# Loads and stores of turns 16 to 30 issued by ScalarE in place of SyncE, in a softmax-attention decode kernel with its gradients

## Chip, cores and metric

The kernel runs on one core of a Trainium2 chip. The metric is the device time of one execution in microseconds (us), the median of several runs. The core has TensorE (PE; its weight loads are PEld), VectorE (DVE), ScalarE (ACT), GpSimd (POOL) and SyncE (SP), and 16 DMA engines that move data between device memory (HBM) and on-chip memory (SBUF). A DMA is issued by an instruction on one of the engines, here `dma_start` on SyncE or ScalarE, and then runs by itself. An engine executes its instructions in order; one that waits for a semaphore holds up all that stand behind it on the same engine.

## What is computed

One query row per head attends to 8192 keys, for 32 heads of width 128, in bf16; the outputs are the attention result and the gradients with respect to q, k and v.

```python
# q, grad_out: [1, 32, 1, 128]; k, v: [1, 32, 8192, 128]; bf16
def _fwd_reference(q, k, v):
    scale = q.shape[-1] ** -0.5
    scores = jnp.einsum('bhqd,bhkd->bhqk', q, k) * scale
    attn = _softmax(scores, axis=-1)
    return jnp.einsum('bhqk,bhkd->bhqd', attn, v)

def reference(q, k, v, grad_out):
    _out, _vjp = jax.vjp(_f, q, k, v)      # _f: _fwd_reference on q, k, v
    return (_out, *_vjp(grad_out))         # out, dq, dk, dv
```

For a head with attention row p and output gradient g this is: out = p V; dp = V g; ds = scale * p * (dp - sum(p * dp)); dq = ds K; dk = outer(ds, q); dv = outer(p, g). K and V are read once (134 MB in all) and dk and dv, of the same size, are written.

## The kernel before

Per head, K, V, dk and dv are each one SBUF tile of 128 partitions x 64 rows x 128 values: 2 MB, 16 KB of neighbouring memory for each partition. Each is one DMA, except K of head 0 (four parts) and the gradients of the first and last head (two halves). There are three K buffers, two V buffers, two buffers for dk (`G_dk`) and two for dv (`G_dv`).

The main loop (L293) makes 33 turns; turn h does the forward part of head h and the gradient of q and k of head h-1 (`p_`). The program has the order of the work written out by hand (`manual_schedule`, L93), so each engine executes its share in the order in which the loop names it. The steps of a turn:

- `rows_bc` (L256) spreads the rows of q and g over the partitions; ScalarE copies them to `qd` (L263).
- `k_blocks` (L150) transposes K in 32x32 blocks on VectorE, `Kt` to `XK_sb` (L155), the first VectorE work of a turn; `k_scores` (L166) multiplies with q on TensorE.
- `ds_of` (L265) makes ds of head h-1 (L268, L270). `outer(p_, "dk", r)`, r = 0 to 3, makes a quarter of dk on VectorE each (L244). `dq_of` (L274, matmuls L221) makes dq in two halves; ScalarE copies the sum to `w_sb` (L228), and `blocks` (L234) and a copy to `dq_all` (L282) finish it.
- Then `load_k(h + 2)` is issued (L314, the DMA is L76): its buffer is that of head h-1, which the second half of `dq_of` reads last.
- The maximum of the scores, `e` = exp and its sum on ScalarE (L333), the sum over partitions (L334), the reciprocal on VectorE (L341) and the scaled `p_rep` on ScalarE (L343). The last quarter of dk stands between, and with it the store of dk of head h-1 (L254).
- `v_transposes` (L191, matmuls L197) turns V in four parts, which ScalarE copies to `XT_sb` (L188); `v_scores` (L209) makes dp; `wide` (L221) and `blocks` (L234) make out, copied at L354.
- `outer(h, "dv", r)`, four quarters of dv on VectorE (L244); before the last of them `load_v(h + 2)` is issued (L364, the DMA is L80), whose buffer is that of V of head h. Behind the last comes the store of dv of head h (L254).

So the DMAs of a turn are, in order: load of K(h+2), store of dk(h-1), load of V(h+2), store of dv(h). SyncE issues all of them and has nothing else to do; each issue waits there until its buffer is free or its data is ready, and the ones behind it wait with it. ScalarE issues one DMA in all, that of `grad_out` (L84). The K and V tiles of heads 0 to 2 are loaded in the prologue and turn 0.

Of the kernel before, what the change touches and what calls it, by code (L numbers as in the profile page):

```python
# [17 lines left out]
K_BUFS = 3  # L18
V_BUFS = 2
QD = 32  # L20


@with_exitstack
def kernel(
# [11 lines left out]
    nc = tc.nc  # L36
# [4 lines left out]
    NCH = NT // CH  # L41
    NQ = P // QD
    assert NCH == 4 and NQ == 4
    W = D // 2
    NB = W // QD
    scale = float(D) ** -0.5
# [15 lines left out]
    Kt, Vt, XK, XV, st = {}, {}, {}, {}, {}  # L62

    def rows_of(x, h, c, parts):
        L = NT // parts
        return x[0, h].rearrange("(p n) d -> p n d", p=P)[:, c * L:(c + 1) * L, :]

    def slots(X, c, parts):
        L = NT // parts
        return X[:, c * L:(c + 1) * L, :]  # L70

    def load_k(h):
        Kt[h] = kpool.tile([P, NT, D], BF16, tag="K", name="Kt")
        parts = NCH if h == 0 else 1
        for c in range(parts):
            nc.sync.dma_start(slots(Kt[h], c, parts), rows_of(k, h, c, parts))  # L76

    def load_v(h):
        Vt[h] = vpool.tile([P, NT, D], BF16, tag="V", name="Vt")
        nc.sync.dma_start(Vt[h][:], rows_of(v, h, 0, 1))  # L80

    rows = consts.tile([H, 2, D], BF16)
    nc.sync.dma_start(rows[:, 0, :], q.rearrange("b h s d -> (b h s) d"))
# [20 lines left out]
    q_blk = consts.tile([P, H, 2 * NB, NQ], BF16)  # L104
    four = consts.tile([H, 2 * NB, NQ, QD], BF16)
    for w in range(NB):
        for e2 in range(2):
            nc.vector.tensor_copy(
                four[:, 2 * w + e2], rows[:, 0, :].rearrange("h (w j e) -> h w e j", w=NB, e=2)[:, w, e2:e2 + 1, :]
                .to_broadcast([H, NQ, QD]))  # L110
    tp = psT.tile([P, CH, P], BF16, tag="T", name="tp_q")
    for c in range(2 * NB):
        nc.tensor.transpose(tp[:, c, 0:H], four[:, c].rearrange("h a j -> h (a j)"), ident[0:H, 0:H])
    lane = consts.tile([P, QD], F32)
    nc.vector.reduce_sum(lane[:], ident[:].rearrange("p (a i) -> p i a", a=NQ), axis=AX.X)
# [4 lines left out]
    nc.vector.reduce_sum(  # L120
        diag_low[:], ident_f[:, 0:3 * QD].rearrange("p (a k r) -> p k r a", a=3, r=R)[:, 0:R, 0, :], axis=AX.X)
    diag = consts.tile([P, R], F32)
# [27 lines left out]
    def k_blocks(h, u):  # L150


        if u == 0:
            XK[h] = ktpool.tile([P, CH, NB, NCH, QD], F32, tag="XK", name="XK_sb")
        nc.vector.transpose(XK[h][:, :, :, u, :],  # L155
                            slots(Kt[h], u, NCH).rearrange("p g d -> p (g d)").bitcast(F32).rearrange(
                                "p (g w j) -> p g w j", g=CH, w=NB))

    def k_scores(h):
        x = st[h]  # L160
        out = x["s"][:, 0:NT].rearrange("p (a g) -> p g a", a=NQ)
        cols = XK.pop(h).rearrange("p g w u i -> p (g w u i)").bitcast(BF16).rearrange(
            "p (g w ui e) -> p g w e ui", g=CH, w=NB, e=2)
        for g in range(CH):
            for c in range(2 * NB):
                nc.tensor.matmul(out[:, g, :], lhsT=cols[:, g, c // 2, c % 2], rhs=q_blk[:, h, c, :],  # L166
                                 start=(c == 0), stop=(c == 2 * NB - 1), skip_group_check=True)
# [69 lines left out]
    def outer(h, which, r):  # L237
        x = st[h]
        if r == 0:
            x[which] = gpool.tile([P, NT, D], BF16, tag=which, name="G_" + which)  # L240
        G, dst = x[which], out_2 if which == "dk" else out_3
        rep, row = x["ds"] if which == "dk" else x["p"], x["qd"][:, 0 if which == "dk" else 1, :]
        Q = NT // 4
        nc.vector.tensor_tensor(  # L244
            slots(G, r, 4).rearrange("p n (a b) -> p n a b", b=R),
            slots(rep, r, 4).unsqueeze(2).to_broadcast([P, Q, D // R, R]),
            row.rearrange("p (a b) -> p a b", b=R).unsqueeze(1).to_broadcast([P, Q, D // R, R]),
            op=ALU.mult)
        parts = 1
        if h == 0 or h == H - 1:  # L250
            parts = 2
        if r % (4 // parts) == 4 // parts - 1:
            c = r // (4 // parts)
            nc.sync.dma_start(rows_of(dst, h, c, parts), slots(G, c, parts))  # L254

    def rows_bc(h):  # L256
        x = st[h]
        x["s"] = psS.tile([P, 512], F32, tag="s", name="s_ps")
        nc.tensor.matmul(x["s"][:, 256:512], lhsT=ident[0:H, h:h + 1].to_broadcast([H, P]),
                         rhs=rows[:].rearrange("h a d -> h (a d)"), start=True, stop=True,  # L260
                         skip_group_check=True)
        x["qd"] = small.tile([P, 2, D], BF16, tag="qd", name="qd")
        nc.scalar.copy(x["qd"][:].rearrange("p a d -> p (a d)"), x["s"][:, 256:512])  # L263
# [10 lines left out]
    def dq_of(h, half):  # L274
        wide(h, "dq", half * NT // 8, (half + 1) * NT // 8)
        if half == 1:
            wide_out(h)

    def dq_out(h):
        out = st[h]["dp"][:, 128:129]  # L280
        blocks(h, out)
        nc.scalar.copy(dq_all[:, h:h + 1], out)  # L282
# [10 lines left out]
    for h in range(H + 1):  # L293
        p_ = h - 1
        if h < H:
            x = st[h] = {}
            rows_bc(h)
            for u in range(NCH):
                k_blocks(h, u)
            k_scores(h)  # L300
        if h == 0:
            do_columns()
        if h > 0:
            ds_of(p_)
            outer(p_, "dk", 0)
            dq_of(p_, 0)
        if h < H:
            s_mask(h)
            s_swap(h)
        if h > 0:  # L310
            dq_of(p_, 1)
            outer(p_, "dk", 1)
        if 0 < h and h + 2 < H:
            load_k(h + 2)  # L314
        if h < H:
            mx = small.tile([P, 1], F32, tag="mx")
            nc.vector.reduce_max(mx[:], x["sn"], axis=AX.X)
            top = small.tile([P, 1], F32, tag="top")
            nc.vector.tensor_scalar_mul(top[:], mx[:], scale)  # L319
            x["m"] = psM.tile([P, 512], F32, tag="m", name="m_ps")  # L320
            nc.tensor.transpose(x["m"][:, 128:256], top[:].to_broadcast([P, P]), ident_f[:])  # L321
        if h > 0:
            outer(p_, "dk", 2)
            dq_out(p_)
        if h == 0:
            load_k(2)
        if h < H:
            nbias = small.tile([P, 1], F32, tag="nbias")
            nc.vector.tensor_reduce(nbias[:], x["m"][:, 128:256], axis=AX.X, op=ALU.max, negate=True)
            v_transposes(h, 0, copy=False)  # L330
            e = small.tile([P, NT], F32, tag="e")
            rs = small.tile([P, 1], F32, tag="rs")
            nc.scalar.activation(e[:], x["sn"], ACT.Exp, bias=nbias[:], scale=scale, accum_out=rs[:])  # L333
            nc.tensor.matmul(x["m"][:, 0:1], lhsT=ones_f[:], rhs=rs[:], start=True, stop=True,  # L334
                             skip_group_check=True)
        if h > 0:
            outer(p_, "dk", 3)
        if h == H:
            break
        rinv = small.tile([P, 1], F32, tag="rinv")  # L340
        nc.vector.reciprocal(rinv[:], x["m"][:, 0:1])  # L341
        x["p"] = small.tile([P, NT, R], BF16, tag="prep", name="p_rep")
        nc.scalar.activation(x["p"][:], e[:].unsqueeze(2).to_broadcast([P, NT, R]), ACT.Copy, scale=rinv[:])  # L343
        x["p_s"] = small.tile([P, NT], F32, tag="p_s", name="p_s")
        nc.vector.tensor_scalar(x["p_s"][:], e[:], rinv[:], scale, op0=ALU.mult, op1=ALU.mult)
        v_copy(h, 0)
        v_transposes(h, 1)
        v_transposes(h, 2)
        wide(h, "o", 0, NT // 4)
        wide_out(h)  # L350
        v_scores(h, 0)
        v_scores(h, 1)
        blocks(h, x["m"][:, 2:3])
        nc.scalar.copy(o_all[:, h:h + 1], x["m"][:, 2:3])  # L354
        v_transposes(h, 3)
        nc.tensor.matmul(x["m"][:, 1:2], lhsT=do_f[:, h:h + 1].to_broadcast([P, P]), rhs=o_all[:, h:h + 1],
                         start=True, stop=True, skip_group_check=True)
        v_scores(h, 2)
        v_scores(h, 3)
        outer(h, "dv", 0)  # L360
        outer(h, "dv", 1)
        outer(h, "dv", 2)
        if 0 < h and h + 2 < H:
            load_v(h + 2)  # L364
        outer(h, "dv", 3)
        if h == 0:
            load_v(2)
        if h == H - 1:
            result(o_all, out_0)
# [33 lines left out]
```

## Time and profile before

| | |
|---|---|
| median of 3 runs | 648.34 us (648.29 to 648.54) |
| profiled execution | 648.14 us, span 646.3 us |
| busy: PE, PEld | 528.0 us (82%), 423.2 us (65%) |
| busy: DVE, ACT | 506.1 us (78%), 214.5 us (33%) |
| moved by DMA | 269.49 MB, mean 417 GB/s |
| mean granted clock of TensorE | 0.684 of full speed |

The span runs from the first to the last instruction of the profiled execution; the rest of that execution's time lies around it. The page of the profile gives the busy time of each engine, a row of 40 slices of the span with the busy share in tenths, the DMA queues with their packets, bytes and share of the 16 engines' span, and the DMA issues by line with the median time from issue to landing. Queue q1 is that of SyncE, q10 that of ScalarE, q8 and q14 fetch instructions. Further views of the same trace: the chain of work that ended last, followed back from the end and shown in order of time (start, duration, what); the waits of an engine (line, what it waited for, total, times, longest); the timeline of one engine (start, duration, instruction, and in brackets the idle time before it with what ended it), where "SPq" marks an instruction that SyncE's sequencer issues; and a table by stretch of time (busy time of PE, PEld, DVE, ACT and POOL with the number of instructions, then granted clock, DMA share and GB/s).

### The profile page before, as it was taken

To read this page: it belongs to the slowest core of one execution; us is meant where nothing else is said; L and a number is where in the kernel's file an instruction comes from. 1 tells how busy PE (TensorE), PEld (TensorE's weight loads), DVE (VectorE), ACT (ScalarE), POOL (GpSimd) and SP (SyncE) were. 2 spreads that over 40 slices of the span, in tenths; PEclk is the share of its full clock that TensorE was granted. 3 is DMA by queue.
4 is the path that set the end of the run, shared out by engine and by line. 5 is a ranking of instruction groups with operands and counts; after the bars stand their busy time and mean duration, and the time that the engine had idled before them with its cause. 6 is when DMAs were issued, how large, how long until landed. Compare 5 with 4: busy or idle time off the path is not lost.

```text
span 646.3 us, 15913 instructions
## 1 busy us (share of the span) xinstructions
PE 528.0 (82%) x7113; PEld 423.2 (65%) x7113; DVE 506.1 (78%) x655; ACT 214.5 (33%) x396; POOL 0.7 (0%) x6
## 2 busy tenths in 40 slices
PE   3988998889899987889877898877897788977781
PEld 3677776766777766667665776656675666766570
DVE  5988888889888778877788777797777977778861
ACT  2334333333343332343313333223432334332340
POOL 0000000000000000000000000000000000000000
PEclk9877665677776656777567765667765777656775
DMA  8999999999999999999999999999999999999984
GB/s 354 399 428 426 425 425 428 424 425 427 427 430 426 429 427 426 429 429 427 429 426 428 428 431 426 427 429 425 429 429 427 427 428 429 427 427 425 423 358 189
DMA packets 19700, 269.49 MB, mean 417 GB/s; under 512 B 2352, under 2 KB 2352, under 8 KB 2864
## 3 DMA queue, kind: packets, MB, share of 16 engines
q1 hardware_dynamic: 19584, 268.47, 98.0%
q8 instruction: 56, 0.92, 0.6%
q14 instruction: 12, 0.10, 0.0%
q10 hardware_dynamic: 48, 0.01, 0.0%
HBM read 134.23 MB, written 134.23 MB: 415 GB/s over the span
## 4 chain that ended last, share of the span: by engine, by line
DMA 49%; DVE 24%; PE 22%; ACT 2%; issue 1%; SPq 0%; ACTq 0%; DVEq 0%
DMA Kt<-in_k_dram 49%; DVE XK_sb L155 15%; DVE G_dv L244 8%; PE w_ps L221 6%; PE s_ps L166 6%; PE T_ps L197 4%; PE dp_ps L234 3%; ACT w_sb L228 1%; ACT p_rep L343 1%; PE s_ps L182 1%; PE m_ps L334 0%; DVE rinv L341 0%; PE dp_ps L209 0%; DVE pdt L268 0%; ACT XT_sb L188 0%
## 5 line engine op out<-in xcount | busy, mean ns | idle before, releaser
L197 PE MATMUL T_ps<-ident_f,Vt 128*128 128x128 f32 x1024 | 202.8, 365 | 1.6 <-ACT XT_sb L188 1.3
L197 PEld LDWEIGHTS T_ps<-ident_f,Vt 128*128 128x128 f32 x1024 | 180.1, 206 | 12.1 <-ACT XT_sb L188 12.1
L244 DVE TENSOR_TENSOR G_dv<-p_rep,qd 128x2048 bf16<-128x2048 bf16 x128 | 148.2, 1220 | 30.5 <-DMA out_dram<-G_dv 27.5
L244 DVE TENSOR_TENSOR G_dk<-ds_rep,qd 128x2048 bf16<-128x2048 bf16 x128 | 155.7, 1218 | 1.1
L155 DVE STREAM_TRANSPOSE XK_sb<-Kt 128x1024 f32<-128x1024 f32 x128 | 148.2, 1213 | 4.9 <-DMA Kt<-in_k_dram 4.6
L188 ACT COPY XT_sb<-T_ps 128x1024 f32<-128x1024 f32 x128 | 128.6, 1008 | 44.5 <-PE T_ps L197 40.8
L166 PE MATMUL s_ps<-q_blk,XK_sb 128*128 128x4 bf16 x2048 | 59.7, 168 | 70.0 <-DVE pdt L268 63.3
L166 PEld LDWEIGHTS <-XK_sb 128*128 128x128 bf16 x2048 | 56.9, 104 | 76.8 <-DVE pdt L268 69.9
L228 ACT COPY w_sb<-w_ps 128x512 f32<-128x512 f32 x64 | 37.6, 587 | 175.5 <-PE w_ps L221 175.4
L209 PEld LDWEIGHTS <-XT_sb 128*128 128x128 bf16 x2048 | 60.7, 98 | 36.9 <-ACT XT_sb L188 23.3
L209 PE MATMUL dp_ps<-do_blk,XT_sb 128*128 128x2 bf16 x2048 | 65.5, 164 | 20.5 <-ACT XT_sb L188 20.5
L234 PEld LDWEIGHTS dp_ps<-diag,w_sb 128*128 128x128 f32 x256 | 56.9, 327 | 17.3 <-ACT w_sb L228 17.3
L221 PE MATMUL w_ps<-Kt,ds_rep 128*32 128x512 bf16 x512 | 67.1, 625 | 0.4 <-DVE ds_rep L270 0.4
L234 PE MATMUL dp_ps<-diag,w_sb 128*128 128x1 f32 x256 | 59.7, 354 | 7.3 <-ACT w_sb L228 7.3
L341 DVE RECIPROCAL rinv<-m_ps 128x1 f32<-128x1 f32 x32 | 5.4, 168 | 70.1 <-PE m_ps L334 70.1
L343 ACT ACTIVATE p_rep<-e,rinv 128x256 bf16<-128x256 f32 x32 | 16.2, 507 | 58.0 <-DVE rinv L341 58.0
L221 PE MATMUL w_ps<-Vt,p_rep 128*32 128x512 bf16 x512 | 34.0, 386 | 0.0
L234 PE MATMUL m_ps<-diag,w_sb 128*128 128x1 f32 x256 | 33.0, 250 | 0.0
L234 PEld LDWEIGHTS m_ps<-diag,w_sb 128*128 128x128 f32 x256 | 31.0, 191 | 0.0
L282 ACT COPY dq_all<-dp_ps 128x1 f32<-128x1 f32 x32 | 5.1, 159 | 62.5 <-PE dp_ps L234 62.5
L321 PEld LDWEIGHTS m_ps<-ident_f,top 128*128 128x128 f32 x32 | 5.8, 182 | 29.0 <-DVE top L319 29.0
L182 PEld LDWEIGHTS s_ps<-sm,lane 128*32 128x32 f32 x256 | 10.4, 151 | 17.5 <-DVE sm L172 16.6
(51 smaller groups left out, 220.9 us busy)
## 6 DMA issues: line engine op xcount, KB each, us to landing
Vt<-in_v_dram SPq DMA_DIRECT2D x32, 2048.0 KB, 29.3
Kt<-in_k_dram SPq DMA_DIRECT2D x31, 2048.0 KB, 31.1
out_dram<-G_dv SPq DMA_DIRECT2D x30, 2048.0 KB, 34.0
out_dram<-G_dk SPq DMA_DIRECT2D x30, 2048.0 KB, 33.8
out_dram<-G_dv SPq DMA_DIRECT2D x4, 1024.0 KB, 15.0
out_dram<-G_dk SPq DMA_DIRECT2D x4, 1024.0 KB, 13.4
Kt<-in_k_dram SPq DMA_DIRECT2D x4, 512.0 KB, 5.2
out_dram<-fin_sb SPq DMA_DIRECT2D x2, 8.0 KB, 12.9
```

The lines of the kernel that those rows point to most:

```text
L155: nc.vector.transpose(XK[h][:, :, :, u, :], slots(Kt[h], u, NCH).rearrange("p g d -> p (g d)").bitcast(F32).rearrange("p (g w j) -> p g w ...
L166: nc.tensor.matmul(out[:, g, :], lhsT=cols[:, g, c // 2, c % 2], rhs=q_blk[:, h, c, :], start=(c == 0), stop=(c == 2 * NB - 1), skip_group ...
L182: nc.tensor.matmul(x["s"][a * QD:(a + 1) * QD, 128:128 + NT], lhsT=lane[:], rhs=x["sm"][:, a].rearrange("p u g -> p (u g)"), start=True, s ...
L188: nc.scalar.copy(X[:], st[h].pop("T")[:])
L197: nc.tensor.transpose(T_ps[:, i, :], words[:, m * P:(m + 1) * P], ident_f[:])
L209: nc.tensor.matmul(st[h]["dp"][:, n:n + 2], lhsT=X[:, i, e2, :], rhs=do_blk[:, h, e2, :], start=(e2 == 0), stop=(e2 == 1), skip_group_chec ...
L221: nc.tensor.matmul(x["w"][a * QD:(a + 1) * QD, :], lhsT=rep[:, n:n + 2 * R, :].rearrange("p n r -> p (n r)"), rhs=Xt[:, 4 * g:4 * g + 4, : ...
L228: nc.scalar.copy(x["wsb"][:].rearrange("p k d -> p (k d)"), x.pop("w")[:])
L234: nc.tensor.matmul(out_col, lhsT=X[:, k, :], rhs=diag[:, k:k + 1], start=(k == 0), stop=(k == R - 1), skip_group_check=True)
L244: nc.vector.tensor_tensor(slots(G, r, 4).rearrange("p n (a b) -> p n a b", b=R), slots(rep, r, 4).unsqueeze(2).to_broadcast([P, Q, D // R, ...
L321: nc.tensor.transpose(x["m"][:, 128:256], top[:].to_broadcast([P, P]), ident_f[:])
L343: nc.scalar.activation(x["p"][:], e[:].unsqueeze(2).to_broadcast([P, NT, R]), ACT.Copy, scale=rinv[:])
```

## The change

A function `issuer(turn)` chooses the engine that issues a DMA: ScalarE for turns 16 to 30, SyncE for all others. The loads and the stores of a turn pass it the number of the turn in which they are issued: h for K and V loads and for the store of dv, and p_ + 1 for the store of dk of head p_. The place of each issue in the program's order stays.

```diff
+FROM, TO = 16, 31
...
-    def load_k(h):
+    def issuer(turn):
+
+        return nc.scalar if FROM <= turn < TO else nc.sync
+
+    def load_k(h, turn=0):
...
-            nc.sync.dma_start(slots(Kt[h], c, parts), rows_of(k, h, c, parts))
-
-    def load_v(h):
+            issuer(turn).dma_start(slots(Kt[h], c, parts), rows_of(k, h, c, parts))
+
+    def load_v(h, turn=0):
         Vt[h] = vpool.tile([P, NT, D], BF16, tag="V", name="Vt")
-        nc.sync.dma_start(Vt[h][:], rows_of(v, h, 0, 1))
+        issuer(turn).dma_start(Vt[h][:], rows_of(v, h, 0, 1))
...
-            nc.sync.dma_start(rows_of(dst, h, c, parts), slots(G, c, parts))
+            issuer(h + 1 if which == "dk" else h).dma_start(rows_of(dst, h, c, parts), slots(G, c, parts))
...
-            load_k(h + 2)
+            load_k(h + 2, h)
...
-            load_v(h + 2)
+            load_v(h + 2, h)
```

## The prediction

> **What bounds the kernel now.** First the page: the DMA row and the queues.
>
> ```profile
> DMA  8999999999999999999999999999999999999984
> q1 hardware_dynamic: 19584, 268.47, 98.0%
> q8 instruction: 56, 0.92, 0.6%
> Vt<-in_v_dram SPq DMA_DIRECT2D x32, 2048.0 KB, 29.3
> out_dram<-G_dk SPq DMA_DIRECT2D x30, 2048.0 KB, 33.8
> ```
>
> The DMA engines are full from the second slice on, nearly all through SP's queue q1. A 2 MB transfer lands some 30 us after its issue, so about six stand in line. Next the chain and the timelines of SP and VectorE, to see how compute hangs on that line:
>
> ```profile
> 206.99 4.53 DVE XK_sb L155 x4
> 294.49 31.18 DMA Kt<-in_k_dram
> 325.69 4.62 DVE XK_sb L155 x4
> ...
> 305.60 0.34 SPq L80 DMA_DIRECT2D Vt<-in_v_dram  x1
> 306.04 0.40 SPq L254 DMA_DIRECT2D out_dram<-G_dv  x1
> 314.42 0.34 SPq L76 DMA_DIRECT2D Kt<-in_k_dram  x1
> 316.81 0.33 SPq L254 DMA_DIRECT2D out_dram<-G_dk  x1
> 325.53 0.34 SPq L80 DMA_DIRECT2D Vt<-in_v_dram  x1
> 334.33 0.34 SPq L76 DMA_DIRECT2D Kt<-in_k_dram  x1
> ...
> 320.85 4.63 DVE L244 TENSOR_TENSOR G_dv<-p_rep,qd 128x2048 bf16<-128x2048 bf16 x4 [1.33 <-DMA out_dram<-G_dv]
> ```
>
> Up to about 207 us a turn takes 18.55 us (chain entries of L155 at 188.50 and 206.99) and the line grows; from then on compute waits for it: K of head 17 (K17) is issued at 294.49, lands at 325.67, and turn 17 starts there. The period is 334.33 - 314.42 = 19.91 us, four transfers of 4.98. Last the end:
>
> ```profile
> SPq L398 <- DMA out_dram<-fin_sb: 12.3, 1, 12.3
> ...
> 630.00:635.00 5.00, 1.78 (x9) 1.51 (x8) 1.90 (x2) 0.63 (x3) 0.00 (x0) 0.50 0.97 402
> 635.00:640.00 5.00, 0.00 (x0) 0.00 (x0) 0.00 (x0) 0.00 (x0) 0.00 (x0) 0.50 0.45 187
> ```
>
> Compute is over at 632.6; SP then waits 12.3 us for the line to empty. So the transfers set the end: it moves later by any time in which the slowest DMA engine has nothing to do, or if compute ends so late that the last store misses the end of the line. The share of 0.45 says that some of the 16 engines finish well before the last one. The profiled execution took 648.14 (span 646.3 and 1.84 around it), the median 648.34; I add differences to the median.
>
> **The change, part by part.** Moved from SP to ScalarE: 14 K loads, 14 V loads, 15 stores of G_dk and 15 of G_dv, 58 issues. Nothing else changes.
>
> *Issue cost.* 0.33 to 0.42 us each on SP; ScalarE's one issue in the trace (grad_out, at 0.73) took 0.42. ScalarE is 33% busy. Where the issues fall in its order:
>
> ```profile
> 334.33 0.59 ACT L228 COPY w_sb<-w_ps 128x512 f32<-128x512 f32 x1 [6.42 <-PE w_ps L221]
> 336.87 0.16 ACT L282 COPY dq_all<-dp_ps 128x1 f32<-128x1 f32 x1 [1.95 <-PE dp_ps L234]
> 336.93 0.32 ACT L333 ACTIVATE e<-s_ps,nbias 128x64 f32<-128x64 f32 x1
> 337.14 0.20 ACT L333 ACTIVATION_READ_ACCUMULATOR e<-s_ps,nbias 128x1 f32 x1
> 339.16 0.51 ACT L343 ACTIVATE p_rep<-e,rinv 128x256 bf16<-128x256 f32 x1 [1.82 <-DVE rinv L341]
> ```
>
> The K load comes behind the w_sb copy and waits for the same matmuls (L221), in the 1.95 us before dq_all. The G_dk store comes behind the read of e's sum and waits for the fourth G_dk multiply (done 336.7), in the 1.82 us before p_rep, which waits for a reciprocal that stands behind that multiply on VectorE anyway. The V load and the G_dv store come behind the last XT copy (ends 326.60); behind them stands the qd copy (327.54), then 6.42 us of idle time. So no wait is added on the path: 58 x 0.4 = 23 us of ScalarE's idle time, price 0. Were that cover gone, it would be 0.4 per turn at p_rep, 15 x 0.4 = 6 us. The transfers themselves start later: K by 0.6, G_dk by 0.6, V and G_dv by 1.1 us. Deep in a line of 30 us that is nothing; with the line empty it counts.
>
> *The crossing at turn 16.* SP's ring holds what was issued before: G_dv14, K17, G_dk14, V17, G_dv15. ScalarE's transfers come through another ring. Do they stand behind SP's line? The fetches of instructions (q8) come in another ring too, 56 times, yet the chain shows 0% of PEq and 1% of issue: they don't wait 30 us. So I let the two rings share, half and half. The numbers on the latest engine, with 1 us from issue to start (an estimate: the 8 KB load of q landed 1.7 us after its issue):
> - K18 starts at about 316. SP's ring then has 24.4 us (G_dv15 landed at 340.7 before); at half speed it lasts till 365.
> - G_dv14 lands at 325 instead of 320.8 and K17 at 335 instead of 325.7. Turn 17 starts 9.6 us late.
> - G_dk14 frees its buffer at 345; VectorE would want it at 340.6. V17 lands at 355 (wanted 351). G_dv15 lands at 365 (wanted 358). Turn 18 starts at about 370 instead of 345.5: compute has lost 24.4 us.
> - ScalarE's ring meanwhile got K18, G_dk15, V18, G_dv16, K19 (ready 350) and G_dk16 (353): 6 x 4.98 = 29.9 us, of which it moved 24.4. At 365 there are 5.4 us left; V19 (ready 366) lasts till 375, G_dv17 (371) till 380.3, K20 (380.3) comes just in time, G_dk17 lasts till 390.2, and V20 is ready at 370 + 19.8 + 1.1 + 1 = 391.8. So the line runs dry for **1.6 us**, 1.1 of which is ScalarE's later issue. Then it grows by 19.91 - 18.55 = 1.36 us per turn.
>
> *The end.* Turn 31 starts at 369.9 + 13 x 18.55 = 611.05 (before 604.82). The last 1 MB store, issued at 631.93 before, goes at about 638.2 and needs 2.5 us and about 1 to start: 641.7, ahead of the line's end (645.2 + 1.6). From turn 31 SP issues again, and G_dk30 (622.1) shares with G_dk29 and G_dv30. G_dk29, 4.9 us of work, lands by 632 and VectorE wants its buffer at 633.5: free.
>
> Sum: 0 + 1.6 + 0 = +1.6: **649.9 us**.
>
> The Trainium skill (DMA: Bandwidth & Descriptors, Rules for kernel authors) says that spreading DMAs over the issuing engines brings no bandwidth, only issue time. SP's four issues take 1.4 of a turn's 19.9 us, so by that rule the time would be 648.3; my 1.6 us come from the order at the crossing, of which the rule doesn't speak. The same page (Queues, rings and completion order) has each DMA engine take its rings in turn, packet by packet, which is the halving assumed above.
>
> *What the trace can't show:* what two full rings do to an engine's rate. Nearest rows: a packet of q1 takes 0.98 x 16 x 646.3 / 19584 = 0.52 us for 13.7 KB (0.62 per 16 KB); a fetch through the other ring 0.006 x 16 x 646.3 / 56 = 1.1 us per 16 KB. Upper end: each of the 80 packets of the shared stretch (2 x 24.4 / 0.61) costs 1.1: +39 us, of which 5 are covered by the slack of the last store: 648.3 + 34 = 682. Lower end: 0, or a small gain (below). I take 0, since the fetch ends in another kind of memory and q1's loads and stores alternate at the full 427 GB/s.
>
> **The rivals.**
> - *Faster: the engines come level again.* The share is 0.90, 0.91, 0.85, 0.83, 0.97, 0.45 in the 5 us stretches from 610 to 640 and 0.05 in the last 6: one engine is late, others are idle. A line that runs nearly dry lets the early ones wait, and the late one may not fall behind again. Bound: not before the last store, 641.7, so 645.2 - 641.7 = 3.5 us less: 644.8 to 647. It decides if lateness comes from a long line rather than from the engine. Against it: nothing shows why that engine is late.
> - *No change, 648.3.* The line never runs dry: 1.6 us is 0.4% of the times it is taken from, and half a transfer more in it at 380 removes it; or rings are served in order of issue.
> - *Two rings cost rate:* 651 to 682 as above; each tenth off the rate in the shared 49 us costs 4.9 on the line.
> - *ScalarE held up:* should an issue there wait longer than the 1.4 us left before p_rep, each further 0.1 us is 1.5 over 15 turns: about 652.
>
> **How the numbers follow.** Dry line 649.9, own range 649.2 to 651: 0.33. No change or under 1.3 us: 0.27. Faster: 0.17. Rate: 0.18. Held up: 0.05. A difference of 0.2% (1.3 us) is what a measurement of this kernel can tell. Slower: 0.18 + 0.05 + three quarters of 0.33 = 0.48; same: 0.27 + 0.08 = 0.35; faster 0.17. The range leaves out the better half of "faster" (below 646.0) and the worse half of "rate" (above 656): 0.17 together.
>
> **What would show it.** In the chain and waits of after: one gap of 4 to 10 us each before L155 (K17), the first G_dk multiply of turn 17, the first T_ps of turn 17 and G_dv of turn 17, all between 320 and 366; none for DMA from turn 18 to 30, which have periods of 18.55; the time to landing near 10 us at turn 19 and growing; a dip in GB/s near 390. p_rep still ends its wait by rinv. The prediction is wrong if K17 lands on time (no sharing), if the GB/s fall between 316 and 365, or if turns 18 to 30 don't run at 18.55.

## The result, and the profile after

The changed kernel takes 653.25 us (median of 4 runs, 652.92 to 653.45), beside 648.44 for the kernel before on the same chip (4 runs). The ratio is 1.0073 with a 95% interval of 1.0055 to 1.009: 4.8 us slower, where 1.6 us had been forecast. The profiled execution took 652.92, of which the span is 651.1.

All line numbers in `kernel.py` are 5 higher than before, because of the added lines: L155 has become L160, L244 L249, L254 L259 and L398 L403.

First the page of the kernel after. The GB/s row has 40 slices of 16.3 us; the queue rows give packets, megabytes and share of the DMA engines' time; the last rows give transfers, KB each and the median time from issue to landing.

```profile
GB/s 352 402 430 423 424 429 425 426 425 429 428 428 425 429 429 429 424 431 429 429 426 429 374 310 398 420 424 427 428 424 428 427 430 425 428 428 427 430 423 206
q1 hardware_dynamic: 11232, 146.83, 53.3%
q10 hardware_dynamic: 8400, 121.65, 44.6%
...
Vt<-in_v_dram ACTq DMA_DIRECT2D x14, 2048.0 KB, 18.9
Kt<-in_k_dram ACTq DMA_DIRECT2D x14, 2048.0 KB, 19.6
out_dram<-G_dk ACTq DMA_DIRECT2D x15, 2048.0 KB, 22.4
out_dram<-G_dv ACTq DMA_DIRECT2D x15, 2048.0 KB, 24.9
```

ScalarE's transfers do have a queue of their own, q10, which now carries nearly half of the work. The slices 23 to 25 (358 to 407 us) show 374, 310 and 398 GB/s: this is the dip that had been placed "near 390", and it is wide. The kernel before has 428, 431 and 426 there.

Now VectorE's timeline of the kernel after. Columns: start, duration, the instruction, and in brackets the idle time ahead of it with what ended it. Only the starts of turns 17 to 19 and the groups that waited for a DMA are shown.

```profile
323.29 4.63 DVE L249 TENSOR_TENSOR G_dv<-p_rep,qd 128x2048 bf16<-128x2048 bf16 x4 [3.76 <-DMA out_dram<-G_dv]
333.00 4.62 DVE L160 STREAM_TRANSPOSE XK_sb<-Kt 128x1024 f32<-128x1024 f32 x4 [5.08 <-DMA Kt<-in_k_dram]
342.99 1.23 DVE L249 TENSOR_TENSOR G_dk<-ds_rep,qd 128x2048 bf16<-128x2048 bf16 x1 [4.74 <-DMA out_dram<-G_dk]
362.83 4.63 DVE L249 TENSOR_TENSOR G_dv<-p_rep,qd 128x2048 bf16<-128x2048 bf16 x4 [7.31 <-DMA out_dram<-G_dv]
367.38 4.62 DVE L160 STREAM_TRANSPOSE XK_sb<-Kt 128x1024 f32<-128x1024 f32 x4
385.93 4.62 DVE L160 STREAM_TRANSPOSE XK_sb<-Kt 128x1024 f32<-128x1024 f32 x4
```

And TensorE's, the first transposes of V in turn 17:

```profile
352.76 1.97 PE L202 MATMUL T_ps<-ident_f,Vt 128*128 128x128 f32 x8 [4.31 <-DMA Vt<-in_v_dram]
```

These are the five waits for SP's half-served line. Turn 18 starts at 367.4 instead of 345.5, so compute has lost 21.9 us; turn 19 follows 18.55 us later and waits for no transfer. The chain of waits of the kernel after says the same. Columns: start, us, what.

```profile
274.58 31.18 DMA Kt<-in_k_dram
305.83 46.88 DMA Vt<-in_v_dram
355.52 7.22 another core or an unknown queue
367.46 4.53 DVE XK_sb L160 x4
386.02 4.53 DVE XK_sb L160 x4
404.58 4.53 DVE XK_sb L160 x4
```

V17 was on its way for 46.88 us, instead of the 30 us usual for SP's line; after the crossing the chain runs through compute at 18.56 us a turn. (The piece put down to an unknown queue ends where G_dv of turn 17 starts; VectorE's timeline above names the transfer.)

The packet records of this trace show the sharing itself. Of the 16 KB packets that start from 317.5 to 342.5 us, 333 go through q1 and 321 through q10; from 342.5 to 360 us it is 97 and 359. One thing more differs from before: SP's last store ahead of the crossing, G_dv15, is issued at 310.91 instead of 306.04, because SP, by its waits, stands 4.7 us for a landing of G_dk. It still stands behind V17 and lands one transfer at half rate after it (352.8 and 362.8), so no effect of this is seen.

Where the lost time is can be read from stretches of 5 us. Columns: the stretch, its length, busy time of PE, PEld, DVE, ACT and POOL with instructions, PE's clock, the share of time in which the 16 DMA engines were busy, and GB/s. Kernel after:

```profile
360.00:365.00 5.00, 3.34 (x61) 3.04 (x57) 2.17 (x2) 1.17 (x2) 0.00 (x0) 0.97 0.78 295
365.00:370.00 5.00, 0.00 (x0) 0.00 (x0) 5.00 (x6) 0.37 (x1) 0.00 (x0) 0.50 1.03 423
370.00:375.00 5.00, 2.95 (x84) 2.39 (x88) 4.72 (x7) 0.00 (x0) 0.00 (x0) 0.50 0.87 367
375.00:380.00 5.00, 4.78 (x29) 3.58 (x22) 3.34 (x6) 1.05 (x4) 0.00 (x0) 0.50 0.71 239
380.00:385.00 5.00, 4.84 (x64) 3.80 (x63) 4.04 (x6) 3.92 (x5) 0.00 (x0) 0.82 1.02 334
385.00:390.00 5.00, 3.48 (x62) 3.09 (x58) 5.00 (x5) 1.56 (x4) 0.00 (x0) 0.86 1.02 377
390.00:395.00 5.00, 4.39 (x89) 2.63 (x89) 4.68 (x9) 0.43 (x1) 0.00 (x0) 0.50 0.96 313
```

Two things lower the rate. From 360 to 365 and from 370 to 380 the share is 0.71 to 0.87: some engines have nothing to do. From 380 to 395 the share is back at 0.96 to 1.02, but the rate is only 313 to 377 GB/s: the engines are busy and move less. By the packet records, 29% of the 16 KB packets that start from 380 to 395 us take more than 0.8 us, against 0.5% from 320 to 360 us; the median is 0.61 us in both stretches.

Why some engines run out first can be read from the landings, of which the trace records 16 for each transfer (one for each engine, as I take it). Around 311 us the first and the last of the 16 lie 8.8 to 8.9 us apart in both kernels. With the line served at half rate this doubles: SP's last transfer, G_dv15, has its landings from 343.9 to 362.7 us. So the first engines are through SP's line 19 us ahead of the last one, go on at full rate with ScalarE's, and reach its end first: the landings of G_dk16 run from 360.4 to 370.1, but the next transfer, V19, is issued only at 362.23. At 418 us the 16 landings of a transfer are 2.7 us apart, against 11.1 before.

The same view in longer stretches gives the balance; the kernel before:

```profile
320.00:360.00 40.00, 32.55 (x447) 26.09 (x446) 31.48 (x40) 13.44 (x25) 0.00 (x0) 0.67 1.01 427
360.00:400.00 40.00, 33.50 (x447) 26.95 (x445) 31.48 (x40) 13.41 (x25) 0.00 (x0) 0.67 1.01 429
400.00:600.00 200.00, 164.54 (x2223) 131.75 (x2222) 157.42 (x200) 66.05 (x122) 0.00 (x0) 0.67 1.01 428
600.00:660.00 60.00, 26.45 (x354) 20.64 (x354) 25.65 (x30) 11.94 (x23) 0.00 (x0) 0.71 0.58 245
```

and after:

```profile
320.00:360.00 40.00, 20.52 (x279) 15.68 (x278) 15.65 (x20) 9.85 (x16) 0.00 (x0) 0.61 1.01 428
360.00:400.00 40.00, 28.57 (x395) 23.32 (x392) 31.37 (x41) 9.72 (x21) 0.00 (x0) 0.64 0.92 346
400.00:600.00 200.00, 177.69 (x2425) 141.67 (x2423) 170.78 (x218) 71.45 (x128) 0.00 (x0) 0.69 1.01 426
600.00:660.00 60.00, 32.00 (x378) 25.41 (x377) 26.91 (x33) 13.84 (x28) 0.00 (x0) 0.67 0.72 303
```

From 320 to 360 the two rings share and the rate is 428 GB/s, as with one. From 360 to 400 the line is short of (429 - 346) / 428 x 40 = 7.8 us of full work. The share falls from 1.01 to 0.92, which accounts for 3.6 us of engines without work; the other 4.2 are engines that are busy and move less. From 400 to 600 another (428 - 426) / 428 x 200 = 0.9 is missing. These 8.7 us are pushed past 600. At the end some comes back: before, 245 x 60 / 428 = 34.3 us of full work took the 45.2 us to the end of the line at 645.2, so 10.9 were lost to engines that finished early; after, 303 x 60 / 428 = 42.5 us of work took 50.0 us, so 7.5 were lost. 8.7 - 3.4 = 5.3 us, beside 4.8 measured. Both kernels move the same bytes, so such a balance has to come out near the measured time; it says where work was lost, not why.

The last landing of each transfer, taken in order and compared with before, says when the end moved: 0.4 us earlier at 370 us, 1.3 later at 387, 2.7 later at 418, 4.7 later at 585, and 4.8 at the end of the line (650.0 and 645.2). So 3.1 us arise between 370 and 418 us, and 2.1 more come slowly over the next 170 us, while the landings of a transfer spread out again from 2.7 to 7.8 us.

The end itself, in SP's timeline of the kernel after, and the wait for the line in its waits:

```profile
627.71 2.60 SPq L259 DMA_DIRECT2D out_dram<-G_dv  x2
637.83 2.60 SPq L259 DMA_DIRECT2D out_dram<-G_dk  x2
640.53 0.41 SPq L296 DMA_DIRECT2D out_dram<-fin_sb  x1
```

```profile
SPq L403 <- DMA out_dram<-fin_sb: 9.1, 1, 9.1
```

The last stores go into a line that still runs for 9.1 us (12.3 before): the transfers, not compute, set the end here too.

### The profile page after: what moved, and what is told of

It is laid out like the page before. It is cut to its first block, busy times and chain, and to the rows that moved or that the text cites. A ratio compares the mean times of both kernels' runs of the same rounds, so it can differ in the third digit from the quotient of the medians.

```text
span 651.1 us, 15890 instructions
## 1 busy us (share of the span) xinstructions
PE 529.7 (81%) x7113; PEld 423.7 (65%) x7113; DVE 504.9 (78%) x655; ACT 214.5 (33%) x396; POOL 0.7 (0%) x6
## 4 chain that ended last, share of the span: by engine, by line
DVE 36%; PE 29%; DMA 27%; ACT 4%; another core or an unknown queue 1%; issue 1%; SPq 0%; DVEq 0%; ACTq 0%
DVE XK_sb L160 18%; DVE G_dv L249 16%; DMA Kt<-in_k_dram 15%; PE s_ps L171 7%; DMA Vt<-in_v_dram 7%; PE w_ps L226 7%; PE T_ps L202 6%; PE dp_ps L239 6%; DMA out_dram<-G_dk 5%; ACT w_sb L233 2%; ACT p_rep L348 2%; PE s_ps L187 1%; PE m_ps L339 1%; DVE rinv L346 1%
## 5 line engine op out<-in xcount | busy, mean ns | idle before, releaser
L202 PEld LDWEIGHTS T_ps<-ident_f,Vt 128*128 128x128 f32 x1024 | 180.5, 206 | 16.3 <-ACT XT_sb L193 11.9
L249 DVE TENSOR_TENSOR G_dv<-p_rep,qd 128x2048 bf16<-128x2048 bf16 x128 | 148.2, 1220 | 26.6 <-DMA out_dram<-G_dv 20.3
L249 DVE TENSOR_TENSOR G_dk<-ds_rep,qd 128x2048 bf16<-128x2048 bf16 x128 | 155.7, 1218 | 9.7 <-DMA out_dram<-G_dk 8.7
L160 DVE STREAM_TRANSPOSE XK_sb<-Kt 128x1024 f32<-128x1024 f32 x128 | 148.2, 1213 | 6.7 <-DMA Kt<-in_k_dram 6.6
L348 ACT ACTIVATE p_rep<-e,rinv 128x256 bf16<-128x256 f32 x32 | 16.3, 508 | 62.5 <-DVE rinv L346 62.5
L287 ACT COPY dq_all<-dp_ps 128x1 f32<-128x1 f32 x32 | 5.1, 159 | 62.5 <-PE dp_ps L239 60.6
```

The costliest lines, as they stand in the source:

```text
L160: nc.vector.transpose(XK[h][:, :, :, u, :], slots(Kt[h], u, NCH).rearrange("p g d -> p (g d)").bitcast(F32).rearrange("p (g w j) -> p g w ...
L202: nc.tensor.transpose(T_ps[:, i, :], words[:, m * P:(m + 1) * P], ident_f[:])
L249: nc.vector.tensor_tensor(slots(G, r, 4).rearrange("p n (a b) -> p n a b", b=R), slots(rep, r, 4).unsqueeze(2).to_broadcast([P, Q, D // R, ...
```

## The experiments

Each is the changed kernel with the edit shown; `FROM` and `TO` are the turns between which ScalarE issues (`TO = 40`: to the end). The kernel before took between 648.12 and 648.23 us beside them, and every ratio is to it.

**ScalarE from the start to the end.** ScalarE issues still more of the transfers, but there is no change of ring while the line is long.

```diff
-FROM, TO = 16, 31
+FROM, TO = 1, 40
```

> FROM, TO = 1, 40: ScalarE issues from turn 1 to the end, so the only crossing lies in turn 1, where the line of transfers is short (about 10 us in place of 25). Theory 'crossing': the loss comes from the new ring overtaking a long line, not from who issues; 648.4 us, between 647.7 and 649.2, XK_sb of turn 17 starts near 325.7 as before. Rival 'issuer': the 4.8 us of turns 16 to 30 are 0.32 us per turn of work held up on ScalarE; with 32 turns 648.4 + 10 = 658.

Measured 646.63 us, ratio 0.9977 (0.9967 to 0.9986): 1.6 us faster than before, and 6.6 faster than the change. The stretch of the dip, in the view by stretches of this kernel:

```profile
360.00:400.00 40.00, 32.75 (x446) 26.06 (x444) 31.48 (x40) 13.40 (x25) 0.00 (x0) 0.67 1.01 429
```

Turn 17 starts at 325.40 after a wait of 0.19 us. So ScalarE as an issuer costs nothing here; the rival by which it does (658) is refuted. The gain had not been expected; its cause stays open.

**One turn on ScalarE.** Only turn 16's four issues cross.

```diff
-FROM, TO = 16, 31
+FROM, TO = 16, 17
```

> FROM, TO = 16, 17: only the four transfers of turn 16 (K18, G_dk15, V18, G_dv16) go through ScalarE's ring. Theory 'crossing': K17, G_dk14 and V17 land as late as with turns 16 to 30 on ScalarE (333, 343, 353 us); G_dv15 about 360 in place of 362.7, since ScalarE's ring is empty after 20 us of work; compute is 2 to 3.5 us earlier, the dry stretch near 380 shorter or gone: 648.5 to 651. Rival 'issuer': one turn of 15 is left: 648.7, and no gaps in turn 17.

Measured 652.06, ratio 1.0064 (1.005 to 1.0077), above what was expected. The waits are nearly those of the full change (K17 5.09, G_dk14 4.72, G_dv15 4.98 us) and the stretch 360 to 400 has 373 GB/s. Four issues out of 58 make 3.8 of the 4.8 us: the price is of the crossing, not of the turns that follow. (The return to SP comes in turn 17 here, while SP's old line is still there; this run doesn't tell the two crossings apart.) By the view by stretches, the share from 360 to 400 us is 0.97, so most of this run's dip is busy engines that move less.

**The crossing late.**

```diff
-FROM, TO = 16, 31
+FROM, TO = 28, 31
```

> FROM, TO = 28, 31: the same crossing 12 turns later, with three turns on ScalarE. Theory 'crossing': turn 30 starts 21.9 us late, as turn 18 did; one turn gives back 1.4 us, so the last store is issued near 652.4 in place of 631.9 and lands 3.5 us later: 11 us more than before, 659 (656 to 662). Rival 'issuer': 3 turns x 0.32 us: 649.4.

Measured 659.42, ratio 1.0175 (1.0161 to 1.0189), as expected. The same waits, three of them here from VectorE's timeline of this kernel:

```profile
572.21 4.62 DVE L160 STREAM_TRANSPOSE XK_sb<-Kt 128x1024 f32<-128x1024 f32 x4 [5.08 <-DMA Kt<-in_k_dram]
582.26 1.22 DVE L249 TENSOR_TENSOR G_dk<-ds_rep,qd 128x2048 bf16<-128x2048 bf16 x1 [4.80 <-DMA out_dram<-G_dk]
602.00 4.63 DVE L249 TENSOR_TENSOR G_dv<-p_rep,qd 128x2048 bf16<-128x2048 bf16 x4 [7.27 <-DMA out_dram<-G_dv]
```

There are no turns left in which compute catches up. The last stores are issued at 649.48 (SP's timeline), and the line ends soon after them (SP's waits):

```profile
649.48 2.60 SPq L259 DMA_DIRECT2D out_dram<-G_dk  x2
```

```profile
SPq L403 <- DMA out_dram<-fin_sb: 3.0, 1, 3.0
```

Here it is compute, late by the crossing, that sets the end.

**The crossing the other way.** ScalarE first, SP from turn 16.

```diff
-FROM, TO = 16, 31
+FROM, TO = 1, 16
```

> FROM, TO = 1, 16: ScalarE issues turns 1 to 15, SyncE from turn 16 on: the crossing at turn 16 in the other direction. Theory 'crossing': the gaps of turn 17 are there as with turns 16 to 30 on ScalarE (K17 lands near 333); issues from turn 17 on are 0.6 to 1.1 us earlier, so the dry stretch is some 1 us shorter, and there is no second crossing in turn 31: 651 to 653.3. Rival 'direction': only ScalarE's ring overtakes, or only its later issues cost: 648.4 and no gaps.

Measured 653.56, ratio 1.0082 (1.0068 to 1.0096), just above what was expected. The waits are the same (5.07, 4.76, 7.34 us), and so is the dip (351 GB/s from 360 to 400). After this crossing SP issues, so the part of the forecast that came from ScalarE's later issue is refuted: the loss is no smaller without it.

**The crossing early, while the line is short,** with the return in turn 31 and without it.

```diff
-FROM, TO = 16, 31
+FROM, TO = 8, 31
```

> FROM, TO = 8, 31: the crossing at turn 8, where K lands 23 us after its issue and is wanted after 28. Theory 'dry line' (the crossing costs only where compute loses so much that the line runs empty or compute ends late): the late landings meet 5 us of slack each, compute loses some 15 us in place of 22, at least 5 us stay in the line, and there are 23 turns to grow it again: no dip in GB/s near turn 10, 647 to 649. Rival 'the crossing itself costs': about 5 us wherever it lies with a line of 20 us or more: 653.

```diff
-FROM, TO = 16, 31
+FROM, TO = 8, 40
```

> FROM, TO = 8, 40: crossing at turn 8, no return to SyncE in turn 31. With TO = 31 the time was 1.2 us above the kernel before, and the last G_dk multiplies waited 4.1 us for a store in ScalarE's ring that shared with SyncE's new ones. Theory 'the return is a second crossing': without it the last multiplies start on time and the time is 0.9 to 1.2 us less: 647 to 648.4. Rival: the 1.2 us come from turn 8; the time stays near 649.3.

Measured 649.36 (ratio 1.0019, 1.0011 to 1.0028) and 649.56 (1.0021, 1.0012 to 1.003), both above what the theory expected. In the first, V9 comes 4.1 us late, G_dk 0.8; the rate stays at 429 and 425 GB/s from 160 to 200 and from 200 to 240, where the kernel before has 428 and 426. The second has 429 and 418, a small dip. A shorter line costs less, though not nothing: 1.2 and 1.4 us. The run without the return to SP is no shorter, so the return is not what costs the 1.2 us.

**Loads alone, and stores alone.** In the first the store line goes back to SP, in the second both load lines.

```diff
-            issuer(h + 1 if which == "dk" else h).dma_start(rows_of(dst, h, c, parts), slots(G, c, parts))
+            nc.sync.dma_start(rows_of(dst, h, c, parts), slots(G, c, parts))
```

> Turns 16 to 30, but only the loads go through ScalarE. Theory 'dry line': K17 still lands near 333, but ScalarE's ring holds half as much, so G_dk14, V17 and G_dv15 land near 340, 345 and 356; turn 18 starts about 15 us late, and SyncE's ring still holds some 15 us of stores then: no dip, 647.7 to 649.5. Rival 'each moved transfer costs its share': 28 of 58, 648.4 + 2.3 = 650.7.

```diff
-            issuer(turn).dma_start(slots(Kt[h], c, parts), rows_of(k, h, c, parts))
+            nc.sync.dma_start(slots(Kt[h], c, parts), rows_of(k, h, c, parts))
...
-        issuer(turn).dma_start(Vt[h][:], rows_of(v, h, 0, 1))
+        nc.sync.dma_start(Vt[h][:], rows_of(v, h, 0, 1))
```

> Turns 16 to 30, but only the stores go through ScalarE. Theory 'dry line': K17 lands near 332, G_dk14 near 340, G_dv15 near 354; turn 18 starts about 15 us late, with some 20 us of loads and stores still in the rings: no dip, 647.7 to 649.5. Rival 'each moved transfer costs its share': 30 of 58, 648.4 + 2.5 = 650.9.

Measured 651.09 (ratio 1.004, 1.0026 to 1.0053) and 651.68 (1.0052, 1.0039 to 1.0064): both above what was expected and nearer to the rival. With loads alone on ScalarE there is no dip; by stretches of that kernel:

```profile
360.00:400.00 40.00, 32.64 (x444) 26.23 (x444) 34.20 (x43) 13.09 (x24) 0.00 (x0) 0.67 1.00 427
```

It loses in another place. The stores on SP's ring take 33 to 34 us from issue to landing, the loads on ScalarE's 18 to 19 (medians of its page). Compute keeps waiting for the stores of G_dv (33.4 us in all, 27.5 before), doesn't catch up, and issues its last stores late (SP's timeline and waits of that kernel):

```profile
640.35 2.60 SPq L259 DMA_DIRECT2D out_dram<-G_dk  x2
```

```profile
SPq L403 <- DMA out_dram<-fin_sb: 5.0, 1, 5.0
```

With stores alone it is K that comes late: K18 holds turn 18 up for 9.94 us, the stretch 360 to 400 has 395 GB/s, and the last wait is 5.2 us. The two halves don't add up to the change; each has an end of its own. That each moved transfer costs its share fits both times, but not the runs with all transfers on ScalarE (faster than before) and with four (+3.8).

**Stores on ScalarE from the first turn to the last.** Both rings always busy, no crossing. Here the load lines are SP's as in the second diff above.

```diff
-FROM, TO = 16, 31
+FROM, TO = 1, 40
```

> Stores from turn 1 to the end through ScalarE, all loads through SyncE: two rings share the engines for the whole time, without a long line being overtaken. Theory 'two rings cost no rate': 647 to 650, 425 to 430 GB/s throughout. Rival 'two rings cost rate': 6.4 us for each per cent, so 655 or more and lower GB/s in every slice.

Measured 649.55, ratio 1.002 (1.0012 to 1.0029), as expected. The rate stays full through the middle:

```profile
280.00:320.00 40.00, 32.69 (x445) 26.39 (x444) 31.21 (x41) 12.92 (x24) 0.00 (x0) 0.67 1.01 428
320.00:360.00 40.00, 33.70 (x448) 26.93 (x448) 32.59 (x42) 13.58 (x25) 0.00 (x0) 0.67 1.01 429
```

Two full rings cost no rate here. K is waited for in 27 turns, 30.6 us in all.

**The change without the return to SP, and the return without the crossing.**

```diff
-FROM, TO = 16, 31
+FROM, TO = 16, 40
```

> FROM, TO = 16, 40: the crossing at turn 16 as before, no return in turn 31. Theory: the dry stretch of 360 to 400 us (346 GB/s against 428) sets the time; the 3.9 us that the last G_dk multiplies waited for the return are covered by the line that is still 9 us long at the end: 652.5 to 653.4. Rival 'return': the late last multiplies are part of the loss: 650 to 651.5.

```diff
-FROM, TO = 16, 31
+FROM, TO = 1, 31
```

> FROM, TO = 1, 31: with TO = 40 the time was 646.6, 1.6 us below the kernel before. Theory 'the return is a second crossing': 1 us more than with TO = 40: 647.4 to 648.2. Rival 'the return costs nothing': 646.6.

Measured 652.96 (ratio 1.0074, 1.0061 to 1.0087) and 646.83 (0.9981, 0.9972 to 0.999). The first has the dip of the change (346 GB/s from 360 to 400) and its time. In the second the last G_dk waits 3.88 us, as the return makes it, and the time is that of the run without it. The return in turn 31 costs nothing that these runs can tell, as its rival in the second expectation had it, so the 4.8 us come from turn 16.

**The crossing in turn 12,** where the line is about as long, with 17 instead of 13 turns behind it.

```diff
-FROM, TO = 16, 31
+FROM, TO = 12, 31
```

> FROM, TO = 12, 31: the crossing at turn 12, where the line is as long as at turn 16 (K13 lands 30.5 us after its issue) and 19 turns go through ScalarE in place of 15. Theory 'dry stretch': the same gaps of turn 17 now in turn 13, the same dip in GB/s some 80 us earlier, and a line that is long again at the end: 652.3 to 653.8, no matter how many turns follow. Rival 'cost per turn on ScalarE': 19/15 of 4.8: 654.4. Rival 'the turns left decide': four more turns give back 5 us: 648.4.

Measured 653.78, ratio 1.0087 (1.0073 to 1.0101). The waits of turn 17 come again in turn 13 (5.09, 4.74, 7.27 us), and so does the dip, 80 us earlier:

```profile
280.00:320.00 40.00, 29.36 (x408) 23.81 (x405) 31.05 (x39) 9.60 (x20) 0.00 (x0) 0.65 0.92 348
```

More turns behind the crossing don't shrink the loss. That the price grows with each turn on ScalarE (654.4) is only 0.6 us away and is excluded by the run with one turn, not by this one.

The rate in the 40 us of the dip and the time above before, side by side:

| ScalarE issues | GB/s in the dip | us above before |
| --- | --- | --- |
| turns 1 to end; 1 to 30 | 429 | -1.6; -1.4 |
| turns 8 to 30; 8 to end | 425, none; 418 | +1.2; +1.4 |
| stores, all turns | 428, none | +1.4 |
| turn 16 alone | 373 | +3.8 |
| turns 16 to 30; 16 to end | 346 | +4.8; +4.8 |
| turns 1 to 15 | 351 | +5.3 |
| turns 12 to 30 | 348 | +5.7 |
| loads of 16 to 30; stores of 16 to 30 | 427; 395 | +3.0; +3.5, by a late end of compute, the second in part by the dip |
| turns 28 to 30 | end of the kernel | +11.2, by a late end of compute |

## Why the prediction was right, and which size was off

The direction was right, and so was most of the mechanism: the rings share, compute comes late, the line runs dry, and the kernel is slower. The term of the sum that was mis-sized is the dry line. Two things were luck. The 653.25 lies outside the 649.2 to 651 given for the dry line; the whole forecast reached up to 656 only for the sake of a rival, that two rings cost rate, which the runs exclude. And 1.1 of the 1.6 us came from a later issue on ScalarE that isn't there: without it the sum would have been 0.5 us, less than the 1.3 that a measurement can tell.

- *Issue cost, price 0: right.* p_rep's waits for rinv grew from 58.0 to 62.5 us, nearly all of it in turn 17, where V17 was late. ScalarE as the only issuer is no slower (646.63).
- *"The transfers themselves start later: K by 0.6, G_dk by 0.6, V and G_dv by 1.1": wrong, and V's made 1.1 of the 1.6 us.* In ScalarE's timeline of the kernel after, the issue of K doesn't wait for the copy ahead of it to end, nor V's for the last copy to `XT_sb` (nor G_dk's, at 378.62, for the activation that starts at 378.61):

```profile
376.01 0.59 ACT L233 COPY w_sb<-w_ps 128x512 f32<-128x512 f32 x1 [7.76 <-PE w_ps L226]
376.02 0.34 ACTq L81 DMA_DIRECT2D Kt<-in_k_dram  x1
...
387.18 1.01 ACT L193 COPY XT_sb<-T_ps 128x1024 f32<-128x1024 f32 x1 [0.83 <-PE T_ps L202]
387.20 0.33 ACTq L85 DMA_DIRECT2D Vt<-in_v_dram  x1
```

- *The crossing: right to some 2 us.* K17 335 forecast and 333.0 measured, G_dk14 345 and 343.0, V17 355 and 352.8, G_dv15 365 and 362.8, turn 18 at 370 and 367.4; 24.4 us lost and 21.9 measured. The halving holds: 333 packets and 321 on the two queues from 317.5 to 342.5 us. (The 24.4 us of line it starts from are 340.7 - 316 = 24.7 by its own figures; that moves nothing else.) The Trainium skill (DMA: Bandwidth & Descriptors, Queues, rings and completion order) has each DMA engine serve its rings in turn, a packet from each; these counts and landings agree with it.
- *The dry line, 1.6 us: mis-sized; the sum needed 4.8.* I reckoned on the latest engine and on one spot, 390.2 to 391.8. By the last landings that spot is worth 3.1 us (370 to 418 us), and 2.1 more come later, for which the sum had no term. Two things are missing in it: the early engines run out from 360 on, long before the latest; and from 380 to 395 us the engines are busy and move less. Over all engines the shortfall is 7.8 us of full work in 360 to 400 and 0.9 later, less 3.4 that come back because the engines finish more evenly (the landings of the last store lie 5.8 us apart, 9.2 before). That last part is the rival "the engines come level again": they do, but it gives back less than was lost.
- *Periods of 18.55 from turn 18: right* (18.56 in the chain; the two entries that the prediction takes it from, 188.50 and 206.99, lie 18.49 apart). *Two rings cost no rate: right,* 428 GB/s from 320 to 360, and 427 to 429 in every stretch from 40 to 600 us with stores on ScalarE throughout. *"Nothing else changes": not quite;* G_dv15 was issued 4.9 us later, to no effect that is seen.
- *The end: the last store ahead of the line's end: right;* issued at 637.83 and 638.2 forecast, with 9.1 us of line behind. *"G_dk29 lands by 632 … free": the landing was wrong, the price right.* It landed at 635.4, and VectorE waited 3.91 us for it, but the run without the return is as long (652.96).

Not settled: without a dip the times still lie between 1.6 us under and 1.4 us above before, and no run tells what sets this; up to so much of the 4.8 us may have another cause than the dip. Why one engine is late, why some packets take longer after a dry spot, and why the last landings fall back another 2.1 us after it, stays open too.

## What to carry to other kernels

Where transfers stand in a long line on one issuer's ring, as here, the place to change the issuer is before the line has formed, or nowhere: transfers on the new ring overtake, the old line is served at half its rate, and its items come late by up to its length (here 22 us out of a 24 us line). What then counts is whether compute has turns left to catch up (13 turns after the late one, 4.8 us; hardly any, 11.2 us) and how long the line is nearly empty meanwhile; reckon that on all engines, since the first of them run out well before the last one, and allow for a lower rate in that stretch. Issuing everything on ScalarE for all turns took 646.6 us here and beat both kernels, by 1.6 and 6.6 us.

## What was unexpected of the hardware

- After a dry spot the DMA engines were busy at a share of 1.02 and moved 334 GB/s, where a share of 1.01 gives 428 with a full line; 29% of the 16 KB packets took more than 0.8 us there, against 0.5%. The kernel before shows it at its start, with a line still short: 342 GB/s at a share of 0.98 from 25 to 30 us.
- ScalarE issued a DMA 0.01 to 0.02 us after the copy ahead of it had started, not after its end.
- The crossing cost about the same in either direction (4.8 and 5.3 us, with overlapping intervals), with the same waits to 0.05 us.
- The 16 landings of one 2 MB transfer were up to 18.8 us apart, and a stretch in which the line ran out brought them within 2.7 us.
- All loads and stores on ScalarE were 1.6 us faster than on SP (ratio 0.9967 to 0.9986), with the same rate in the middle, 429 GB/s.
